# The last 64 keys' scores of two heads: one matmul over the whole array, or one per head in half of the array

## The chip, the cores and the metric

The kernel runs on one core of one Trainium2 chip. The metric is the device time of the program in microseconds (us), the median of several runs; smaller is better. The engines go by the names of the profile: PE is TensorE's matmul part, PEld its weight loads (they overlap PE), ACT is ScalarE, DVE is VectorE, POOL is GpSimd, SP is the engine that issues most transfers. SBUF is the working memory; PSUM is the memory that TensorE writes its results to, in eight banks of 512 f32 values per partition.

## The reference

Two stages, all in f32. The first is attention with 8 batches, 8 heads, 576 positions and head size 64, in which every query keeps only its 32 largest scores:

```
scores = scale * np.matmul(q, k.transpose(0, 1, 3, 2))
kth = np.partition(scores, -top_k, axis=-1)[..., -top_k:-top_k + 1]
scores = np.where(scores >= kth, scores, -1000000000.0)
attn = softmax(scores)          # max subtracted, 1e-9 added to the sum
out = np.matmul(attn, v)
```

The second is an MLP over the 4608 rows of 512 values which that gives: x times w_in (512 x 2048), the exact gelu, times w_out (2048 x 512).

## The kernel before

**Tiles.** Two heads form a pair, 32 pairs in all. The 576 positions are four blocks of 128 and a last part of 64 (TL). An item is one block of 128 queries of one pair (128 items), or the last 64 queries of two pairs together (16 items, t == NM). For each pair, transpose_qk (L238) puts q and k, transposed, into a tile qk: partitions 0 to 63 hold head 0, partitions 64 to 127 head 1. Columns KT and up hold the first 512 keys of both heads. Columns SM + P to KT are the last keys: 128 columns, where the first 64 belong to head 0 and the other 64 to head 1. The raw tile was zero outside the two heads' own corners, so in those columns head 0's rows are zero for head 1's keys and the other way round.

**Scores (L280).** For an item of 128 queries, TensorE makes t_ps at L290: one matmul over all 128 rows of the array, whose 128 columns are the last-key scores of both heads at once, thanks to the zeros. Then L294 makes s_ps, two PSUM banks, one per head: four matmuls of 256 columns, each over the 64 rows of its head, so that two heads can go through the two halves of the array at the same time. An f32 matmul is two passes in the trace, each with its own weight load. ScalarE then copies s_ps (L298, 1024 columns) and t_ps (L299, 128 columns) into the item's score tile s in SBUF, with the scale. The row of s is laid out as head 0's 512 keys, head 0's last 64, head 1's last 64, head 1's 512 keys, so that each head's 576 scores are in one piece.

**The loop (L609).** One trip per item, with several items in different stages: scores of item n + 2, the product with V of item n - 3 (attend, L440, matmuls at L458 or L468 into the tile o), the softmax of item n - 1 on ScalarE (L380 and L381), transposes of the weights of item n - 2 (tp_t at L409, two tp at L427, copied by ScalarE at L410 and L434), top_k of item n on VectorE (L341, L344), and the normalisation of item n - 1 on POOL (L392). Between these stand pieces of the MLP (mlp, L576): l1_piece (L499, h_ps), the gelus on ScalarE (L513), l2_piece (L534, y_ps), and the copy of a finished y (L548). In a trip with attend, which is every second trip for the items of 128 queries, the matmuls of o follow those of the scores directly; else a piece of the MLP follows.

**What sets the order.** Each engine runs its instructions in the order of this program text (manual_schedule). Semaphores make one engine wait for another, and all that stands behind a waiting instruction on its engine waits too.

**PSUM.** The eight banks are: two for s_ps (tag "s", one buffer), two for the tag "tp", two for h_ps and two for y_ps. The tag "tp" is shared by t_ps, o, the transposes tp_t, tp and tp_qk:

```
s_ps = ps.tile([P, 2, 512], f32, tag="s", bufs=1, name="s_ps")
t_ps = ps.tile([P, 512], f32, tag="tp", name="t_ps")
...
o = ps.tile([P, 512], f32, tag="tp", name="o")
```

Each new tile of a tag takes the bank of the tile that came two before it, and its first matmul waits until that one's last reader is done.

Of the kernel before, what the change touches and what calls it, by code (L numbers as in the profile page):

```python
# [14 lines left out]
def kernel(  # L15
# [19 lines left out]
    nc = tc.nc  # L35
    f32, i32, u32 = mybir.dt.float32, mybir.dt.int32, mybir.dt.uint32
    bf16, i16, u16 = mybir.dt.bfloat16, mybir.dt.int16, mybir.dt.uint16
    AF = mybir.ActivationFunctionType
    ALU = mybir.AluOpType

    B, H, S, D = q.shape
    P = 128
# [5 lines left out]
    SM = NM * P  # L48
    TL = S - SM
# [6 lines left out]
    scale = 1.0 / float(D) ** 0.5  # L56
# [5 lines left out]
    ps = ctx.enter_context(tc.tile_pool(name="ps", bufs=2, space=bass.MemoryType.PSUM))  # L62
# [172 lines left out]
    KT = SM + 2 * P  # L235
# [31 lines left out]
    def spread(t, step, n):  # L267

        return bass.AP(tensor=t.tensor, offset=t.offset, ap=[list(t.ap[0]), [step, 2], [1, n]])

    def half(r, e):


        return slice((r ^ e) * TL, ((r ^ e) + 1) * TL)
# [5 lines left out]
    def scores(i):  # L280
        if i >= N:
            return
        pair, t = items[i]
        S_of[i] = s = work.tile([P, 2 * S], f32, tag="s", bufs=5, name="s")
        s_ps = ps.tile([P, 2, 512], f32, tag="s", bufs=1, name="s_ps")
        t_ps = ps.tile([P, 512], f32, tag="tp", name="t_ps")
        if t < NM:
            qk = qk_of[pair]
            lhsT = qk[:, t * P : (t + 1) * P]
            nc.tensor.matmul(t_ps[:, 0:P], lhsT=lhsT, rhs=qk[:, SM + P : KT], start=True, stop=True)  # L290
            for c in range(2):
                for e in range(2):
                    rows = slice(e * D, (e + 1) * D)
                    nc.tensor.matmul(  # L294
                        s_ps[:, e, c * 256 : (c + 1) * 256], lhsT=lhsT[rows, :],
                        rhs=qk[rows, KT + c * 256 : KT + (c + 1) * 256], start=True, stop=True,
                    )
            nc.scalar.activation(spread(s, S + TL, SM), s_ps, func=AF.Copy, scale=scale)  # L298
            nc.scalar.activation(s[:, SM : S + TL], t_ps[:, 0:P], func=AF.Copy, scale=scale)  # L299
        else:  # L300
            for r in range(2):
                qk = qk_of[pair + r]
                for e in range(2):
                    nc.tensor.matmul(
                        t_ps[half(r, e), r * TL : (r + 1) * TL],
                        lhsT=qk[:, SM + e * TL : SM + (e + 1) * TL],
                        rhs=qk[:, SM + P + e * TL : SM + P + (e + 1) * TL],
                        start=True, stop=True,
                    )

            for r in range(2):
                qk = qk_of[pair + r]
                for e in range(2):
                    rows = slice(e * D, (e + 1) * D)
                    nc.tensor.matmul(  # L315
                        s_ps[half(r, e), r, :], lhsT=qk[rows, SM + e * TL : SM + (e + 1) * TL],
                        rhs=qk[rows, KT:], start=True, stop=True,
                    )
            s2 = s.rearrange("p (r n) -> p r n", r=2)
            nc.scalar.activation(s2[:, :, 0:SM], s_ps, func=AF.Copy, scale=scale)  # L320
            nc.scalar.activation(
                s2[:, :, SM:S], t_ps[:, 0:P].rearrange("p (r n) -> p r n", r=2),
                func=AF.Copy, scale=scale,
            )
# [270 lines left out]
    for pair in range(2):  # L595
        for piece in transpose_qk(pair, pair == 0):
            piece()
        if pair == 0:
            scores(0)
            scores(1)  # L600
# [8 lines left out]
    for n in range(ahead):  # L609

        left[0] = 7 if n < START + 2 * NP else 8
        weights_add(unit_in(n))
        scores(n + 2)
        product = attend(n - 3)
        late = n > START
# [71 lines left out]
```

## Time and profile before

| what | value |
|---|---|
| time, median of 3 runs | 1713.43 us (1713.32 to 1719.77) |
| PE busy | 1612.4 us, 94% |
| DVE busy | 1428.2 us, 83% |
| ACT busy | 1189.2 us, 69% |
| L290, t_ps | 256 passes, 53.4 us |
| L294, s_ps | 1024 passes, 154.5 us |
| L298, copy of s_ps | 128 times, 1028 ns each |
| L299, copy of t_ps | 128 times, 278 ns each |
| L548, copy of y | 36 times, 603 ns each |

How to read the profile: busy time is the time in which an engine has an instruction running, and matmuls overlap one another, so their busy times do not add up to the time they cost; the distance from one group's start to the next group's start does. A line of the table of groups names the source line, the engine, the tiles (out<-in), the shape, how often, then the busy time and the mean of one. A line of the table of waits reads "engine tile line <- who ended the wait: us in total, times, longest". A line of the timeline is start, length, engine, line, operation, tiles and how many were merged; in brackets stands the idle time before it and what ended it.

### The profile page before, as it was taken

How to read it: one execution, taken by the hardware profiler on the slowest of the kernel's cores; microseconds unless marked ns; L12 is line 12 of the kernel's file. 1: busy time of each engine (PE TensorE's matmuls, PEld its weight loads, DVE VectorE, ACT ScalarE, POOL GpSimd, SP SyncE). 2: the span in 40 equal slices, each digit the busy share in tenths (PEclk: the TensorE clock that was granted, in tenths of full speed). 3: DMA queues.
4: the chain of work that ended last, by engine and by line, in shares of the span. 5: the costliest groups of instructions: out<-in, count | busy, mean ns of one | idle time of the engine just before them, and what ended most of it. 6: DMA issues, size and time to landing. Idle time of an engine off the chain costs nothing.

```text
span 1713.1 us, 24404 instructions
## 1 busy us (share of the span) xinstructions
PE 1612.4 (94%) x8480; PEld 1093.2 (64%) x8480; DVE 1428.2 (83%) x3042; ACT 1189.2 (69%) x2147; POOL 663.0 (39%) x764
## 2 busy tenths in 40 slices
PE   5558999999999999999999999999999999999999
PEld 3336567766666667666666667676666666766665
DVE  6998989988799887998889888898889987899900
ACT  5877876767676767776767776776777776777730
POOL 3667833333233332333333323333333333333310
PEclk8669999999999999999999999999999999999999
DMA  5422210011100111002100011001110010000000
GB/s 157 133 99 87 84 48 1 13 27 24 40 13 1 41 29 41 1 13 49 28 27 1 27 42 41 1 14 27 29 48 1 13 29 15 21 1 13 7 13 13
DMA packets 126715, 56.10 MB, mean 33 GB/s; under 512 B 117888, under 2 KB 117888, under 8 KB 126592
## 3 DMA queue, kind: packets, MB, share of 16 engines
q1 hardware_dynamic: 125056, 52.16, 11.4%
q0 software_dynamic: 320, 2.10, 0.3%
q8 instruction: 67, 1.10, 0.3%
q14 instruction: 56, 0.46, 0.1%
q10 hardware_dynamic: 1216, 0.30, 0.1%
HBM read 45.08 MB, written 9.44 MB: 32 GB/s over the span
## 4 chain that ended last, share of the span: by engine, by line
PE 83%; ACT 6%; POOL 0%; issue 0%; ACTq 0%; POOLq 0%
PE h_ps L506 27%; PE y_ps L542 27%; PE o L458 8%; PE s_ps L294 7%; PE tp L427 6%; PE o L468 2%; PE t_ps L290 1%; PE tp_qk L249 1%; ACT s L381 1%; ACT L381 1%; ACT s L380 1%; PE s_ps L315 1%; PE tp_t L409 1%; ACT L517 1%; ACT g L517 1%; ACT pt L434 0%
## 5 line engine op out<-in xcount | busy, mean ns | idle before, releaser
L341 DVE MAX8 top<-rest 128x8 f32<-128x576 f32 x864 | 612.5, 754 | 0.0
L506 PE MATMUL h_ps<-xT,w_in_sb 128*128 128x256 f32 (+1 forms) x2560 | 559.3, 363 | 4.3 <-ACT g L517 4.3
L542 PE MATMUL y_ps<-w_out_sb,g 128*128 128x512 f32 x1152 | 546.1, 598 | 0.0
L392 POOL TENSOR_SCALAR s<-s,rden 128x576 f32<-128x576 f32 x288 | 493.6, 1723 | 0.8 <-issue 0.4
L506 PEld LDWEIGHTS h_ps<-xT,w_in_sb 128*128 128x128 f32 x2560 | 430.3, 192 | 66.6 <-issue 15.8
L344 DVE MATCH_REPLACE8 rest<-top,rest 128x576 f32<-128x576 f32 x576 | 425.4, 750 | 0.0
L373 POOL TENSOR_SCALAR den<-den 128x2 f32<-128x2 f32 x144 | 32.0, 222 | 884.0 <-ACT s L381 883.4
L542 PEld LDWEIGHTS y_ps<-w_out_sb,g 128*128 128x128 f32 x1152 | 196.2, 190 | 173.2 <-issue 172.7
L298 ACT ACTIVATE s<-s_ps 128x1024 f32<-128x1024 f32 x128 | 131.6, 1028 | 189.7 <-PE s_ps L294 189.7
L381 ACT ACTIVATE s<-s,bias 128x576 f32<-128x576 f32 x288 | 223.3, 775 | 12.8
L380 ACT ACTIVATE s<-s,neg 128x576 f32<-128x576 f32 x288 | 223.8, 777 | 1.6 <-POOL neg L356 1.1
L434 ACT COPY pt<-tp 128x512 f32<-128x512 f32 x256 | 147.3, 576 | 109.2 <-PE tp L427 108.5
L427 PEld LDWEIGHTS tp<-ident,s 128*128 128x128 f32 x1152 | 147.0, 145 | 118.5 <-issue 57.6
L344 DVE MATCH_REPLACE8 rest<-top,s 128x576 f32<-128x576 f32 x288 | 212.4, 748 | 0.0
L341 DVE MAX8 top<-s 128x8 f32<-128x576 f32 x288 | 202.4, 747 | 5.1 <-ACT s L299 5.1
L427 PE MATMUL tp<-ident,s 128*128 128x128 f32 x1152 | 179.6, 281 | 28.3 <-ACT qk L253 13.7
L367 DVE RECIPROCAL rden<-den 128x2 f32<-128x2 f32 x144 | 23.7, 164 | 194.2 <-POOL den L373 194.2
L294 PE MATMUL s_ps<-qk 64*128 64x256 f32 x1024 | 154.5, 423 | 3.5 <-ACT s L298 3.5
L458 PE MATMUL o<-pt,raw_v 128*64 128x256 f32 x1280 | 153.6, 387 | 2.1 <-ACT pt L434 2.1
L458 PEld LDWEIGHTS o<-pt,raw_v 128*64 128x64 f32 x1280 | 86.8, 138 | 66.9 <-issue 17.9
L294 PEld LDWEIGHTS s_ps<-qk 64*128 64x128 f32 x1024 | 92.9, 196 | 27.1 <-ACT s L298 4.0
L517 ACT ACTIVATE g<-h_ps 128x512 f32<-128x512 f32 x144 | 78.6, 595 | 37.8 <-PE h_ps L506 37.1
(65 smaller groups left out, 1106.6 us busy)
## 6 DMA issues: line engine op xcount, KB each, us to landing
raw_q<-in_q_dram SPq DMA_DIRECT2D x64, 128.0 KB, 2.3
raw_v<-in_v_dram SPq DMA_DIRECT2D x64, 128.0 KB, 2.4
out_dram<-y SPq DMA_DIRECT2D x32, 256.0 KB, 2.2
raw_k<-in_k_dram SPq DMA_DIRECT2D x62, 128.0 KB, 2.4
w_out_sb<-in_moe_w_in_dram SPq DMA_DIRECT2D x12, 511.8 KB, 4.7
w_out_sb<-in_moe_w_out_dram SPq DMA_DIRECT2D x10, 511.8 KB, 4.0
w_out_sb<-in_moe_w_in_dram POOLq DMA_DIRECT2D x4, 511.8 KB, 8.6
words<-in_moe_w_out_dram SPq DMA_DIRECT2D x4, 511.8 KB, 5.0
```

The lines of the kernel that those rows point to most:

```text
L294: nc.tensor.matmul(s_ps[:, e, c * 256 : (c + 1) * 256], lhsT=lhsT[rows, :], rhs=qk[rows, KT + c * 256 : KT + (c + 1) * 256], start=True, s ...
L298: nc.scalar.activation(spread(s, S + TL, SM), s_ps, func=AF.Copy, scale=scale)
L341: nc.vector.max(st["top"][:, e, 8 * r : 8 * r + 8], cur[e])
L344: nc.vector.match_replace(rest[:, e], st["top"][:, e, 8 * r : 8 * r + 8], cur[e], LOWEST)
L380: nc.scalar.activation(s, s, func=AF.Prelu, bias=st["neg"][:, e, 1:2], scale=1.0, alpha=STEEP)
L381: nc.scalar.activation(s, s, func=AF.Exp, bias=st["bias"][:, e : e + 1], scale=1.0, accum_out=st["den"][:, e : e + 1],)
L392: nc.gpsimd.tensor_scalar(s, s, st["rden"][:, e : e + 1], None, op0=ALU.mult)
L427: nc.tensor.transpose(tp[:, j * P : (j + 1) * P], s[:, first + j * P : first + (j + 1) * P], ident)
L434: nc.scalar.copy(out=dst, in_=tp.rearrange("p (j n) -> p j n", j=NM))
L458: nc.tensor.matmul(o[e * D : (e + 1) * D, 0:n], lhsT=vt[:, j, e, :], rhs=pt[:, e * NM + j if j < NM else 2 * NM, :], start=(j == 0), stop= ...
L506: nc.tensor.matmul(h_tile(u)[:, i, :], lhsT=w_in_sb[:, ko, f * P : (f + 1) * P], rhs=xT[:, ko, c0 : c0 + n], start=(ko == 0), stop=(ko == ...
L542: nc.tensor.matmul(y_of[sub], lhsT=g_of[u][:, i, sub * P : (sub + 1) * P], rhs=w_out_sb[:, f, :], start=(f == 0), stop=(f == FT - 1),)
```

## The change

The scores of the last keys are made per head. Each head's 64 columns come from a matmul over the 64 rows of that head alone, so all six matmuls of an item use one half of the array. Two halves may not write one PSUM bank at the same time, so each head's tail has a bank of its own: t_ps for head 0, the new t1_ps for head 1, both from the tag "tp". The order on TensorE is head 0's tail, then the four mains beginning with head 1 and alternating, then head 1's tail, so that the two halves have the same work. ScalarE makes three copies in place of two: head 0's tail first, then the 1024 columns of s_ps, then head 1's tail. It is meant to use both halves fully: the whole-array matmul, half of whose products are with zeros, goes away. Items of the last 64 queries (t == NM) are as before.

```diff
-            nc.tensor.matmul(t_ps[:, 0:P], lhsT=lhsT, rhs=qk[:, SM + P : KT], start=True, stop=True)
-            for c in range(2):
-                for e in range(2):
-                    rows = slice(e * D, (e + 1) * D)
-                    nc.tensor.matmul(
-                        s_ps[:, e, c * 256 : (c + 1) * 256], lhsT=lhsT[rows, :],
-                        rhs=qk[rows, KT + c * 256 : KT + (c + 1) * 256], start=True, stop=True,
-                    )
+            t1_ps = ps.tile([P, 512], f32, tag="tp", name="t_ps")
+            tails = [
+                (e, dst[:, 0:TL], SM + P + e * TL, TL) for e, dst in enumerate((t_ps, t1_ps))
+            ]
+            mains = [
+                (e, s_ps[:, e, c * 256 : (c + 1) * 256], KT + c * 256, 256)
+                for c in range(2) for e in (1, 0)
+            ]
+            for e, dst, at, n in tails[:1] + mains + tails[1:]:
+                rows = slice(e * D, (e + 1) * D)
+                nc.tensor.matmul(
+                    dst, lhsT=lhsT[rows, :], rhs=qk[rows, at : at + n], start=True, stop=True
+                )
+            nc.scalar.activation(s[:, SM:S], t_ps[:, 0:TL], func=AF.Copy, scale=scale)
             nc.scalar.activation(spread(s, S + TL, SM), s_ps, func=AF.Copy, scale=scale)
-            nc.scalar.activation(s[:, SM : S + TL], t_ps[:, 0:P], func=AF.Copy, scale=scale)
+            nc.scalar.activation(s[:, S : S + TL], t1_ps[:, 0:TL], func=AF.Copy, scale=scale)
```

## The prediction, made before the changed kernel ran

> **What bounds the kernel now.** I read the page's busy times and slices first, then the waits of each engine, then the timeline around single score tiles.
>
> ```profile
> PE 1612.4 (94%) x8480; PEld 1093.2 (64%) x8480; DVE 1428.2 (83%) x3042; ACT 1189.2 (69%) x2147; POOL 663.0 (39%) x764
> ...
> PE   5558999999999999999999999999999999999999
> ...
> DVE  6998989988799887998889888898889987899900
> ACT  5877876767676767776767776776777776777730
> ```
>
> From slice 6 on (about 215 us) TensorE (PE) is full. Before that VectorE (DVE) is: the table of windows gives it 43.00 us busy in 43:86 and again in 86:129. So after 215 us a stop of TensorE lengthens the run; from 43 to 129 it does not, as long as VectorE is fed. That the later part does not hang on VectorE is in its waits, the first of these lines; the second tells how often ScalarE (ACT) is early or late for the scores.
>
> ```profile
> DVE rden L367 <- POOL den L373: 194.2, 98, 8.7
> ...
> ACT s L298 <- PE s_ps L294: 189.7, 97, 5.2
> ```
>
> VectorE waits 194.2 us in all. ScalarE waited for TensorE at 97 of the 128 score evictions; at the other 31 it arrived late. What it was doing then is in the timeline. First a tile where a gelu stood ahead of the scores, ScalarE from 674 us (the scores began on TensorE at 674.49):
>
> ```profile
> 674.76 1.08 ACT L517 ACTIVATE g<-h_ps 128x512 f32<-128x512 f32 x2
> 676.05 1.02 ACT L298 ACTIVATE s<-s_ps 128x1024 f32<-128x1024 f32 x1 [0.20 <-PE s_ps L294]
> 676.97 0.27 ACT L299 ACTIVATE s<-t_ps 128x128 f32<-128x128 f32 x1
> ```
>
> Then a tile where a finished output y was copied too, on both engines:
>
> ```profile
> 651.35 1.08 ACT L517 ACTIVATE g<-h_ps 128x512 f32<-128x512 f32 x2
> 652.32 1.08 ACT L548 COPY y<-y_ps 128x512 f32<-128x512 f32 x2
> 653.26 1.07 ACT L298 ACTIVATE s<-s_ps 128x1024 f32<-128x1024 f32 x1
> ```
>
> ```profile
> 650.66 0.59 PE L542 MATMUL y_ps<-w_out_sb,g 128*128 128x512 f32 x1
> 651.09 0.38 PE L290 MATMUL t_ps<-qk 128*128 128x128 f32 x2
> 651.40 1.14 PE L294 MATMUL s_ps<-qk 64*128 64x256 f32 x8
> 652.47 2.50 PE L468 MATMUL o<-ptt,raw_v 128*128 128x128 f32 x20
> ```
>
> The reader is to see this: TensorE goes from the scores (651.09) to the product with V (o, 652.47) after 1.38 us and does not care that ScalarE reaches these scores only at 653.26. In the first case it reaches them at about 675.84 (end of the second gelu), 1.35 us after the scores began.
>
> **What the skill says, and the trace.** "TensorEngine Tiling (Array Packing)", Key Properties: a change of the tiling mode drains TensorE. The trace agrees: from t_ps (128 rows) to s_ps (64 rows) takes 0.31 us where two passes of 128 columns need 2 x 0.109 (four transposes of L427 take 0.44 until the next group starts), so 0.09 is drain. The same page, Gotcha 1: different row tiles cannot use one PSUM bank at once; that is why each head's tail now needs its own bank. "TensorE: Matmul & The Clock Gate", LDWEIGHTS: the load takes columns/1.2 ns, 107 ns for 128 columns, however few rows. The pitch of 0.109 us agrees, though matmul and load need the same time there, so it does not tell them apart.
>
> **The change, part by part.**
>
> TensorE's work. The page counts 256 instructions at L290 for 128 tiles, so an f32 matmul is two passes, each with its own weight load. Before: two passes of 128 columns, 0.218; drain 0.096; then from 651.40 to o at 652.47, 1.065: the eight L294 passes run as four pairs of the two row halves, 4 x 0.216 = 0.864 (0.216 is the pitch of 256 columns: L506's four in 0.87), and the 0.20 left I split into the first weight load, which nothing hides behind a drain, 0.104, and the drain out, 0.097. Sum 1.379; the timeline has 1.38. After: no 128-row matmul, six 64-row ones. The mode changes stay two, only the first stands before the tails. Each half now carries one tail of two passes plus two mains of two. A tail pass streams 64 columns, 0.054, but its successor's 128-column load needs 0.107 and can start only as the pass starts. I take 0.107 per tail pass, and 0.054 and a full serialisation as the ends. One half: 2 x 0.107 + 4 x 0.216 = 1.078; with drain in 0.096, first load 0.104, drain out 0.097: 1.375. So TensorE gains 0.004 us per tile, 0.5 us in all: the removed full-array matmul comes back as loads.
>
> ScalarE's work. One 128x128 eviction (278 ns at L299) becomes two of 128x64. "ScalarE: Activation LUTs", What ACT_TABLE_LOAD costs, gives 186 ns + 0.833 ns per element, 239 at 64; at 128 it gives 293 where the trace has 272 median, so I scale from the trace: 272 - 53 = 219. That is 0.16 us more per tile, 20 us over 128 tiles, of which nearly all lies in ScalarE's idle time: the first tail's eviction goes ahead of the wait for s_ps. After the mains only one of 219 stands where one of 272 stood.
>
> The buffers. This is the part that costs. The tag "tp" has two banks, and each new tile of it takes the bank of the tile before last. Before: scores took one (A), and the o after it took B, last read by the copy at L434, which ScalarE had done before the gelu. After: scores take A and B, o takes A, so o waits for the eviction of the first tail. That eviction is queued on ScalarE behind the gelus and y copies of the block before. Behind o, in TensorE's order, stand all later matmuls, so nothing fills the wait. From ScalarE's end to TensorE's start a release takes 0.05 (timeline, the copy at L253 to L427).
>
> How long, tile by tile after 215 us. o stands straight behind these scores in 64 cases, and alternates with tiles that have MLP pieces first (next user of "tp" 2.3 us or more after the start, against about 0.9 for the first tail's eviction: no wait). In twelve of the 64 ScalarE is not late. 34 have only gelus: the eviction starts at 1.35 - 0.115 (a copy starts that much ahead of the end of the gelu before it: 652.32 against 652.43) = 1.237 after the start, ends at 1.456, o starts at 1.51 in place of 1.375: 0.13 each, 4.5 us. 18 have y copies (36 of 603 ns in the table of groups, four of them after the last scores): in 14 with two of them the eviction starts at 653.26 - 651.09 = 2.17, o at 2.45: 1.07 each, 15.0 us; in 4, with one, at 1.70, o at 1.97: 0.59 each, 2.3 us. Together 22 us. After the delayed o ScalarE waits for o anyway (L474 idle 0.50 in the y case), so the next tile starts equally late and nothing is made up.
>
> Before 215 us ScalarE is late by 2 to 4 us at most tiles (weight conversion), and o waits up to 2 us five times; four of these fall in windows where VectorE is full, the one at 150 us can cost up to 2. I take 1.
>
> The second bank's wait, tail 1 on the last L434 copy, is hidden by the four mains ahead of it and by MLP pieces. Result: 1713.4 - 0.5 + 22 + 1 = 1736.
>
> **Rivals.**
> 1. Tail passes cost only their 64 columns (0.054). Then a tile is 0.107 shorter where o does not wait for ScalarE: some 60 tiles, 6 us; where it waits, the time of o is ScalarE's. 1736 - 6 = 1730. For it: L304, 64 columns with 64-column loads, runs its pairs fast. Against: those loads are half as wide.
> 2. The halves do not overlap once they are out of step: about 0.13 more per tile, again only where o does not wait: 1736 + 8 = 1744. For it: pairs ran in step in the trace before. Against: four quarter tiles at L315 overlap freely, eight passes of 512 columns in 1.02 us.
> 3. No net wait: o's stop is taken from waits TensorE has anyway. Time 1714. For it: TensorE's waits add up to 97 us. Against: 42 of them are L409 on POOL before 170 us, and what recurs later (L427 on L253, 2.1 us a time) stands in the few tiles with a new pair's transposes.
> 4. Faster: rival 1 on all 128 tiles and no wait for the tail bank, 1713.4 - 13.7 = 1700. It needs two of my steps wrong.
>
> **How the numbers follow.** Main case 0.62, rival 1 0.13, rival 2 0.12, rival 3 0.08, rival 4 0.05. Slower by over 0.5% (above 1722) is the main case and rivals 1 and 2, 0.87; same 0.08; faster 0.05. The range runs from rival 1 less some microseconds for the eviction's length and the release, 1725, to rival 2 plus the early phase's 2 us, 1747; rivals 3 and 4 stay outside with 0.13.
>
> **What would show it.** In the waits of TensorE: o at L458 and L468 behind the new first tail's eviction, about 50 times after 215 us, 22 us, the longest 1.1. Timeline from the first tail to o: 1.38 us where ScalarE is free, 1.5 behind gelus, 2.4 behind y copies. A tile's six matmuls as long as the five before means the load bound holds; 1.27 means rival 1, 1.5 everywhere rival 2. VectorE's wait at L367 grows. I am wrong if o starts at 1.38 behind a late ScalarE, or if TensorE's later waits shrink by as much as these grow.

## The result, and the profile after

The changed kernel takes 1742.77 us (median of 5 runs, 1738.42 to 1743.92), the kernel before 1714.55 beside it. The ratio is 1.0154, with a 95% interval of 1.0133 to 1.0176: slower by about 28 us. In the changed kernel the six matmuls of an item stand at L302, the three copies at L305 (first tail), L306 (s_ps) and L307 (second tail). All lines behind them moved by 8: o is now L466 and L476, the MLP's L514 and L550, the gelu L525, the copy of y L556.

The busy times of the page hardly tell what happened. TensorE is as full as before, in a longer span:

```profile
PE 1619.0 (93%) x8736; PEld 1102.1 (63%) x8736; DVE 1428.5 (82%) x3042; ACT 1203.1 (69%) x2275; POOL 662.5 (38%) x764
...
PE   5558999999999999999999999999999999999999
```

The table of waits does (engine, tile and line <- who ended the wait: us in total, times, longest). TensorE's, of the kernel after:

```profile
PE o L466 <- ACT s L305: 21.4, 19, 2.5
...
PE o L476 <- ACT s L305: 4.2, 4, 1.1
```

No such line was there before. The 25.6 us count only stops that outlast the modelled end of the last matmul; short ones show in the weight loader, where o waits for L305 57 times.

VectorE's waits took up what TensorE lost, 223.3 us where there were 194.2, so VectorE was not what held the kernel:

```profile
DVE rden L375 <- POOL den L381: 223.3, 101, 8.7
```

The timeline of one tile with two y copies, the counterpart of the one shown before, first ScalarE, then TensorE (start, length, engine, line):

```profile
661.93 1.08 ACT L525 ACTIVATE g<-h_ps 128x512 f32<-128x512 f32 x2
662.90 1.08 ACT L556 COPY y<-y_ps 128x512 f32<-128x512 f32 x2
663.84 0.27 ACT L305 ACTIVATE s<-t_ps 128x64 f32<-128x64 f32 x1
663.95 1.07 ACT L306 ACTIVATE s<-s_ps 128x1024 f32<-128x1024 f32 x1
```

```profile
661.75 0.32 PE L302 MATMUL t_ps<-qk 64*128 64x64 f32 x1
...
662.02 0.86 PE L302 MATMUL s_ps<-qk 64*128 64x256 f32 x6
...
662.78 0.27 PE L302 MATMUL t_ps<-qk 64*128 64x64 f32 x1
664.16 2.50 PE L476 MATMUL o<-ptt,raw_v 128*128 128x128 f32 x20 [1.06 <-ACT s L305]
```

TensorE has its last score matmul under way at 662.78 and stands until 664.16, 0.05 after the first tail's copy ends at 664.11. ScalarE came to that copy only after the gelus and the copies of y. Where ScalarE is free, the same distance, from the first tail to o, is 1.28 us (650.07 to 651.35):

```profile
650.07 0.32 PE L302 MATMUL t_ps<-qk 64*128 64x64 f32 x1
...
651.35 2.50 PE L476 MATMUL o<-ptt,raw_v 128*128 128x128 f32 x20
```

Over the run after 215 us the distance takes four values: 1.28 where ScalarE is free, 1.43 behind gelus (34 times), 1.92 behind gelus and one copy of y (4 times), 2.41 behind two (14 times). One tile, at 224 us, stands apart: it waits 2.1 us for the copy at L442, as its counterpart before waited for that at L434.

### The profile page after: what moved, and what is told of

It reads as the page before. It is cut to its first block, busy times and chain, and to the rows that moved or that the text cites. A ratio compares the mean times of both kernels' runs of the same rounds, so it can differ in the third digit from the quotient of the medians.

```text
span 1741.4 us, 25044 instructions
## 1 busy us (share of the span) xinstructions
PE 1619.0 (93%) x8736; PEld 1102.1 (63%) x8736; DVE 1428.5 (82%) x3042; ACT 1203.1 (69%) x2275; POOL 662.5 (38%) x764
## 3 DMA queue, kind: packets, MB, share of 16 engines
q8 instruction: 69, 1.13, 0.3%
## 4 chain that ended last, share of the span: by engine, by line
PE 66%; ACT 20%; issue 2%; POOL 0%; ACTq 0%; POOLq 0%
PE h_ps L514 27%; PE y_ps L550 17%; PE o L466 8%; PE tp L435 5%; ACT L525 4%; ACT g L525 3%; ACT pt L442 3%; PE s_ps L302 3%; ACT s L389 3%; ACT s L388 3%; PE o L476 2%; PE tp_qk L249 1%; PE t_ps L302 1%; ACT L389 1%; ACT y L556 1%
## 5 line engine op out<-in xcount | busy, mean ns | idle before, releaser
L514 PE MATMUL h_ps<-xT,w_in_sb 128*128 128x256 f32 (+1 forms) x2560 | 559.8, 363 | 5.5 <-ACT g L525 5.5
L550 PE MATMUL y_ps<-w_out_sb,g 128*128 128x512 f32 x1152 | 546.1, 598 | 0.0
L514 PEld LDWEIGHTS h_ps<-xT,w_in_sb 128*128 128x128 f32 x2560 | 430.6, 192 | 67.7 <-issue 19.4
L550 PEld LDWEIGHTS y_ps<-w_out_sb,g 128*128 128x128 f32 x1152 | 196.2, 190 | 162.6 <-issue 156.5
L389 ACT ACTIVATE s<-s,bias 128x576 f32<-128x576 f32 x288 | 223.3, 775 | 13.0
L442 ACT COPY pt<-tp 128x512 f32<-128x512 f32 x256 | 147.4, 576 | 110.2 <-PE tp L435 109.5
L375 DVE RECIPROCAL rden<-den 128x2 f32<-128x2 f32 x144 | 23.1, 160 | 223.3 <-POOL den L381 223.3
L302 PE MATMUL s_ps<-qk 64*128 64x256 f32 x1024 | 182.4, 417 | 1.0 <-ACT s L306 1.0
L466 PE MATMUL o<-pt,raw_v 128*64 128x256 f32 x1280 | 155.7, 390 | 23.8 <-ACT s L305 21.4
L306 ACT ACTIVATE s<-s_ps 128x1024 f32<-128x1024 f32 x128 | 131.7, 1029 | 43.3 <-PE s_ps L302 43.0
L302 PEld LDWEIGHTS t_ps<-qk 64*128 64x128 f32 x512 | 90.1, 196 | 80.9 <-issue 57.2
L466 PEld LDWEIGHTS o<-pt,raw_v 128*64 128x64 f32 x1280 | 87.8, 139 | 80.9 <-ACT s L305 33.0
L302 PEld LDWEIGHTS s_ps<-qk 64*128 64x128 f32 x1024 | 119.6, 197 | 6.6 <-ACT s L306 1.4
```

The lines of the kernel that those rows point to most:

```text
L302: nc.tensor.matmul(dst, lhsT=lhsT[rows, :], rhs=qk[rows, at : at + n], start=True, stop=True)
L389: nc.scalar.activation(s, s, func=AF.Exp, bias=st["bias"][:, e : e + 1], scale=1.0, accum_out=st["den"][:, e : e + 1],)
L442: nc.scalar.copy(out=dst, in_=tp.rearrange("p (j n) -> p j n", j=NM))
L466: nc.tensor.matmul(o[e * D : (e + 1) * D, 0:n], lhsT=vt[:, j, e, :], rhs=pt[:, e * NM + j if j < NM else 2 * NM, :], start=(j == 0), stop= ...
L514: nc.tensor.matmul(h_tile(u)[:, i, :], lhsT=w_in_sb[:, ko, f * P : (f + 1) * P], rhs=xT[:, ko, c0 : c0 + n], start=(ko == 0), stop=(ko == ...
L550: nc.tensor.matmul(y_of[sub], lhsT=g_of[u][:, i, sub * P : (sub + 1) * P], rhs=w_out_sb[:, f, :], start=(f == 0), stop=(f == FT - 1),)
```

## The experiments

Three explanations had to be told apart. The theory: the second tail takes a bank of the tag "tp", so that o gets the bank of the first tail and waits for its copy on a late ScalarE. Rival A: ScalarE's third copy costs by itself. Rival B: the half-array matmuls cost by themselves. Each ratio below is taken against runs of the kernel before made beside the experiment; their median stands with it.

**The matmuls alone.** Edit against the changed kernel:

```diff
-            nc.scalar.activation(s[:, SM:S], t_ps[:, 0:TL], func=AF.Copy, scale=scale)
             nc.scalar.activation(spread(s, S + TL, SM), s_ps, func=AF.Copy, scale=scale)
-            nc.scalar.activation(s[:, S : S + TL], t1_ps[:, 0:TL], func=AF.Copy, scale=scale)
+            nc.scalar.activation(s[:, SM : S + TL], s_ps[:, 0, 0:P], func=AF.Copy, scale=scale)
```

> Keeps the six half-array matmuls in their two tail banks, but ScalarE copies as in the kernel before: s_ps, then one copy of 128 columns, taken from s_ps in place of the tails. The tails' scores are thus left out of the result; the work of every engine is else that of the change. The second bank is free as soon as it is written. Theory (o waits for the first tail's copy, behind a late ScalarE): no wait of o, 1714 us, within 3 of the kernel before. Rival A (ScalarE's third copy costs): also 1714. Rival B (the half-array matmuls cost): 1743, as the changed kernel.

Measured: 1717.31 against 1713.65 us, ratio 1.0013 (1.0000 to 1.0025). Rival B is out as the cause: by the ratio the matmuls cost 2 us, at most 4, of the 28. In the trace not even these look to be theirs: the distance from the first tail to o is 1.28 us in 63 of the 64 tiles after 215 us. The trace has four stretches of 3.41 us after 215 us in which TensorE ran at half its clock, where that of the kernel before has one (more on such stretches below). No wait of o for a copy of the scores is left in TensorE's table; the one line on o is this:

```profile
PE o L465 <- ACT pt L441: 1.3, 1, 1.3
```

**The copies alone.** Edit against the kernel before:

```diff
+            nc.scalar.activation(s[:, SM:S], t_ps[:, 0:TL], func=AF.Copy, scale=scale)
             nc.scalar.activation(spread(s, S + TL, SM), s_ps, func=AF.Copy, scale=scale)
-            nc.scalar.activation(s[:, SM : S + TL], t_ps[:, 0:P], func=AF.Copy, scale=scale)
+            nc.scalar.activation(s[:, S : S + TL], t_ps[:, TL:P], func=AF.Copy, scale=scale)
```

> The matmuls and the one bank of the kernel before; only the tail's copy is cut in two of 64 columns, the first ahead of the copy of s_ps. Theory: ScalarE's 20 us more lie in its idle time, o takes the bank that was free before: 1714 to 1716. Rival A: 1730 to 1743. Rival B: 1714.

Measured: 1713.25 against 1713.65 us, ratio 1.0001 (0.9993 to 1.0008). Rival A is out. The two small copies are there, at 231 and 227 ns, but they lie in time in which ScalarE waited: the wait ahead of the scores' copies is now in two parts.

```profile
ACT s L298 <- PE t_ps L290: 111.4, 59, 3.7
...
ACT s L299 <- PE s_ps L294: 51.7, 63, 1.9
```

163.1 us where the kernel before had 189.7.

**The bank alone, first attempt.** The copies of the tail and of s_ps change places, and one more tile is taken:

```diff
+            ps.tile([P, 512], f32, tag="tp", name="t_ps")
...
+            nc.scalar.activation(s[:, SM : S + TL], t_ps[:, 0:P], func=AF.Copy, scale=scale)
             nc.scalar.activation(spread(s, S + TL, SM), s_ps, func=AF.Copy, scale=scale)
-            nc.scalar.activation(s[:, SM : S + TL], t_ps[:, 0:P], func=AF.Copy, scale=scale)
```

> The matmuls of the kernel before, two copies as before but the 128 columns of the tail ahead of s_ps; and one more tile of the tag tp is taken in each score tile and never used, so that o gets the bank of t_ps. Theory: o waits for that copy as in the changed kernel, behind gelus 0.2 us, behind y copies 1.15: 1740 to 1748. Rivals A and B: 1714.

Measured: 1713.28 against 1713.65 us, ratio 0.9996 (0.9987 to 1.0004): a miss, but no evidence against the theory. Its trace has no wait of o for the tail, which fits that the unused tile got no bank and o went where it had gone before. The run is of use as a control: to copy the tail ahead of s_ps costs nothing by itself.

**The banks swapped.** The tile t1_ps is taken ahead of t_ps in the changed kernel:

```diff
+        if t < NM:
+            t1_ps = ps.tile([P, 512], f32, tag="tp", name="t_ps")
         t_ps = ps.tile([P, 512], f32, tag="tp", name="t_ps")
...
-            t1_ps = ps.tile([P, 512], f32, tag="tp", name="t_ps")
```

> The changed kernel with the two tail banks taken in the other order, so that o gets the bank of the tail that is copied last. Theory: every o that stands behind scores waits for the last copy: about 1.3 us more where ScalarE is free (12 times), 1.15 behind gelus (33), 1.03 behind y copies (18), 72 us in all: 1800 to 1820. Rivals A and B: 1743, since no work is added.

Measured: 1738.89 against 1713.65 us, ratio 1.0143 (1.0129 to 1.0156), as the change itself. Again the edit did not do what I meant: the trace still shows o behind the first tail's copy (L304 here). With the run before it this fits that a tile gets its bank at its first use, not where it is taken; and the first tail is still written first.

```profile
PE o L465 <- ACT s L304: 20.6, 19, 2.0
```

**The bank alone, with a tile that is used.** Edit against the kernel before:

```diff
+            nc.scalar.activation(s[:, SM : S + TL], t_ps[:, 0:P], func=AF.Copy, scale=scale)
             nc.scalar.activation(spread(s, S + TL, SM), s_ps, func=AF.Copy, scale=scale)
-            nc.scalar.activation(s[:, SM : S + TL], t_ps[:, 0:P], func=AF.Copy, scale=scale)
+            pad = ps.tile([P, 512], f32, tag="tp", name="pad")
+            nc.scalar.copy(out=pad[:, 0:2], in_=ident[:, 0:2])
```

> As the run of the bank alone, but the second tile of the tag is used (ScalarE writes two columns of it after the scores), since a tile that no instruction touches got no bank: in this program o goes to the bank of t_ps. Matmuls as before the change, the 128 columns of the tail copied ahead of s_ps. Theory: o waits for that copy as in the changed kernel: 1738 to 1748. Rivals A (ScalarE's third copy) and B (half-array matmuls): 1714.

Measured: 1742.61 against 1717.26 us, ratio 1.0153 (1.0131 to 1.0174). The whole loss is there without one half-array matmul and with the tail copied in one piece. From the first attempt, which lost nothing, this kernel differs in the tile that is used and ScalarE's copy of two columns into it; that a third small copy on ScalarE costs nothing was shown by the copies alone. Its waits of o are those of the change:

```profile
PE o L460 <- ACT s L298: 23.8, 20, 2.3
...
PE o L470 <- ACT s L298: 4.4, 4, 1.1
```

**The first tail copied last.** This is what the swap of banks was to show. In the changed kernel the copy of t_ps goes behind the other two:

```diff
-            nc.scalar.activation(s[:, SM:S], t_ps[:, 0:TL], func=AF.Copy, scale=scale)
             nc.scalar.activation(spread(s, S + TL, SM), s_ps, func=AF.Copy, scale=scale)
             nc.scalar.activation(s[:, S : S + TL], t1_ps[:, 0:TL], func=AF.Copy, scale=scale)
+            nc.scalar.activation(s[:, SM:S], t_ps[:, 0:TL], func=AF.Copy, scale=scale)
```

> The changed kernel with the copy of the first tail moved behind the two others on ScalarE; no work is added. Theory: o, which goes to that tail's bank, waits for all three copies: about 1.3 us more where ScalarE is free (12 times), 1.15 behind gelus (33), 1.03 behind y copies (18), 72 us in all: 1800 to 1820. Rivals A and B: 1743.

Measured: 1845.81 against 1717.26 us, ratio 1.0753 (1.0730 to 1.0776). No work was added, a copy was moved, and 103 us more were lost than by the change. The time is above the 1800 to 1820 expected. The waits of o are now

```profile
PE o L466 <- ACT s L306: 80.9, 53, 2.8
...
PE o L476 <- ACT s L306: 23.3, 16, 2.0
```

104.2 us in place of 25.6, which is 78.6 more. The distance from the first tail to o became 2.64 where ScalarE is free or behind gelus, 2.84 behind one copy of y and 3.33 behind two: 1.36, 1.21 and 0.92 more, where I had 1.3, 1.15 and 1.03. Tile by tile that is 73 us after 215 us, so the 72 expected came true. The traces of the two kernels differ by 102 us. Of the other 29, 10 arise before 215 us. Most of what is left goes with the clock: after 215 us this trace has 13 stretches of 3.41 us at half the clock, that of the changed kernel has two. At some 1.7 us each, an estimate from those measured below, eleven more cost 18 us. Other users of the tag wait longer too (transposes of a new pair behind L306 8.2 us, tp_t behind L307 8.0), but their waits add little after 215 us.

**o ahead of the scores.** In the changed kernel:

```diff
-        scores(n + 2)
         product = attend(n - 3)
+        scores(n + 2)
```

> The changed kernel with the product with V ahead of the scores in each trip, so that ScalarE has the 2.3 us of o to finish its gelus and copies before the first tail is there. Theory: the waits of o for a tail go; the scores reach ScalarE 2.3 us later, so the softmax starts about 0.8 us later in these trips, which VectorE's waits should take up: 1714 to 1728. Rivals A (third copy) and B (half-array matmuls): 1743, since all work stays.

Measured: 1739.81 against 1714.11 us, ratio 1.0134 (1.0112 to 1.0155). The waits of o for a tail are gone from the table, as the theory has it, and yet the time is not back. The same move in the kernel before tells why:

> The kernel before with the product with V ahead of the scores, as the run that put o first did for the changed kernel. If that run's 25 us came from the order alone, this one is slow as well, 1735 to 1740. If they come from the two tail banks, whose next users now wait for the scores' copies in the trips with a new pair's transposes, this one is at 1710 to 1716.

Measured: 1751.59 us, ratio 1.0203 (1.0181 to 1.0226), with its own runs of the kernel before at 1717.26. The order costs by itself, more than the wait that it takes away, so these two runs say nothing against the theory, and my expectation for the first was wrong. Besides, they show where half-array tails pay. The tiling mode of a group, the rows and columns of the array that one matmul uses, stands ahead of its tiles' sizes in the timeline. With o first, what stands ahead of the scores is often in the mode 128*64, and the old order of scores then changes mode once more: into 128*128 for t_ps, then into 64*128. The changed kernel goes to 64*128 at once. First the kernel before with o first, then the changed one:

```profile
730.16 2.38 PE L458 MATMUL o<-pt,raw_v 128*64 128x256 f32 x20
732.47 0.49 PE L290 MATMUL t_ps<-qk 128*128 128x128 f32 x2
732.89 1.13 PE L294 MATMUL s_ps<-qk 64*128 64x256 f32 x8
733.95 0.38 PE L506 MATMUL h_ps<-xT,w_in_sb 128*128 128x128 f32 x1
```

```profile
721.19 2.38 PE L466 MATMUL o<-pt,raw_v 128*64 128x256 f32 x20
723.50 0.32 PE L302 MATMUL t_ps<-qk 64*128 64x64 f32 x1
...
724.78 1.49 PE L514 MATMUL h_ps<-xT,w_in_sb 128*128 128x128 f32 x11
```

From the start of o to the group behind the scores it is 3.79 us and 3.59. The 0.20 recurs behind every o in the mode 128*64 after 215 us but one, 47 times, together 9.4 of the 12 us between the two runs. Behind an o in the mode 128*128 (L468 and L476, 16 trips) both kernels take about 3.61. What the order itself costs was not taken apart further.

**The gelus one piece sooner.** In the changed kernel, so that ScalarE is less late:

```diff
-    GELU_AT = 5
+    GELU_AT = 4
```

> The changed kernel with GELU_AT 4 in place of 5: the gelus go to ScalarE one piece of the MLP sooner, ahead of the last transposes' copy, so that ScalarE comes to the scores about 0.7 us earlier. Theory: no wait of o behind gelus, about 0.4 left behind two y copies, the early part's 4 us stay: 1720 to 1730. Rivals A and B: 1743.

Measured: 1850.14 against 1717.26 us, ratio 1.0777 (1.0752 to 1.0802). My expectation failed. The gelus now stand ahead of the last copy of a trip's transposes (L442), and TensorE waits for that copy's bank as it starts the scores. One wait was traded for a larger one, and its trace has 17 stretches of 3.41 us at half the clock after 215 us, where the changed kernel's has two. So this run cannot tell how the lateness of ScalarE scales the loss:

```profile
PE t_ps L302 <- ACT pt L442: 54.9, 45, 1.2
...
PE o L466 <- ACT s L305: 14.8, 19, 1.9
```

## Why the prediction was right

**The bank, the main step.** Right, and shown by two runs: the bank without the matmuls gives the whole loss, the matmuls without the bank's copies none that matters. The count was right as well (14, 4 and 34 tiles). The sizes were a little low: 0.15 for 0.13 behind gelus, 1.13 for 1.07 behind two y copies, 0.64 for 0.59 behind one. Sum 23 us for 22. In the y case I had taken 0.219 us for a 64-column copy; there it takes 0.27, and 0.224 in the median.

**Nothing made up.** Right. A transpose of the last trips, at 1639.33 us before, starts at 1667.60 after, 28.3 later; one at 215.31 starts at 219.55, 4.2 later. So 24 of the 28 us come after 215 us, and the waits of o account for 23 of them. What is left is the clock, for which the prediction had no term. Twice after 215 us the changed kernel's TensorE ran 3.41 us at half its clock (from 369.31 and 1280.67 us), the kernel before once (from 454.03); each time it fell back by about 1.7 us. In the windows (columns: stretch, its length, busy us of PE, PEld, DVE, ACT and POOL with counts, granted clock as a share of the full one, DMA share, GB/s), first after, then before:

```profile
369.40:372.60 3.20, 3.20 (x12) 2.74 (x13) 0.97 (x2) 2.13 (x4) 0.00 (x0) 0.50 0.00 0
```

```profile
454.10:457.30 3.20, 3.20 (x12) 2.56 (x11) 1.00 (x4) 2.55 (x5) 0.95 (x4) 0.50 0.00 0
```

These are the profiled executions; in others their number may differ.

**TensorE's work.** Right: I had 1.375 us in place of 1.379. Measured: the drain in, 0.096 (L550's six passes to L302 2.67 where 2.577 was usual), then 1.28, so 1.376. The sign that I had given, 1.38 from the first tail to o and 1.27 for rival 1, was set wrong: in the new order the drain lies ahead of the first tail, so from there my own sum is 1.279 and rival 1's is 1.17. The 1.28 measured is mine. In trips without a wait of o nothing was gained or lost, three apart that gained 0.20. That the first half's tail passes are bound by their weight loads fits the timeline of the y case: t_ps at 661.75, the first main of its half (merged into the line at 662.02) at 662.08, 0.33 later: two loads of 0.107 and the 0.104 or so that the first load costs. Rival 1 would have had 0.21 there. The two halves, out of step by a tail, did not slow each other, which is against rival 2.

**ScalarE's work.** Right, shown by the copies alone.

**The part before 215 us.** Here is most of the miss, 4.2 us where I took 1. The step that failed is "the one at 150 us can cost up to 2. I take 1". o waits there 1.89 us, at the bound I gave, and then runs slowly. The windows of the kernel after:

```profile
151.90:154.00 2.10, 0.31 (x3) 0.17 (x2) 2.10 (x3) 2.07 (x4) 2.04 (x2) 1.00 0.00 0
154.00:158.20 4.20, 4.10 (x21) 2.26 (x21) 4.20 (x11) 1.08 (x3) 4.12 (x3) 0.59 0.01 4
```

After the stop the granted clock of TensorE is 0.59 for the stretch, and the product o takes 4.07 us; before, it took 2.38 at the full clock:

```profile
151.60 2.38 PE L458 MATMUL o<-pt,raw_v 128*64 128x256 f32 x20
```

The Trainium skill, "TensorE: Matmul & The Clock Gate", HAM oscillation, gives as the rule no idle gaps of TensorE above about 3.4 us. Here a stop of 1.89 us was enough, and the measurement decides. The other runs bear this out: where o stops at this place for 1.89 to 2.06 us (banks swapped, bank alone with a used tile, gelus sooner), 3.4 us at half the clock follow; where it does not stop (matmuls alone, copies alone, first attempt), the clock stays at 1.00. The four other late tiles before 130 us cost nothing that lasted: at 126 us the changed kernel was 0.36 us behind, since VectorE was the bound there.

So the forecast of 1736 fell short by 7 us: some 3 from the early part, 1 from the sizes of the waits, 1.1 since the kernel before itself measured higher in these runs, and 1 to 2 from one more stretch at half the clock. The last comes from single traces, the 7 from medians.

**A version better than both** did not come of it. Both tails in one bank would free o, but the two halves' matmuls would then write one bank with nothing to order them. That was not tried.

## What to carry to other kernels

Before adding a tile to a shared PSUM tag, list who takes its banks next and which copy frees them: a matmul that was free of ScalarE may come to stand behind everything ScalarE has queued. Splitting a copy off for an early start does not help if the engine that makes it is late just then. A matmul of few columns over half the array need not be cheaper: here a tail's two passes cost the time of their weight loads, and they paid only where they saved a change of tiling mode. When two runs differ by more than the waits explain, compare the granted clock along both traces.

## What the hardware showed beyond that

- Passes of the two row halves of the array start independently: in the y case s_ps of one half starts at 661.76 beside the other half's tail at 661.75, and at the end t_ps of one and s_ps of the other both start at 662.72, with no loss against the sum for one half (1.376 measured, 1.375 worked out).
- One more change of tiling mode costs 0.20 us a time (3.79 in place of 3.59, 47 times). An estimate of its parts: 0.10 until the array is drained, from 2.67 less 2.577, and the other 0.10 for a first weight load that nothing hides.
- A stop of 1.89 us was followed by 3.4 us at half the clock, which nearly doubled its cost. Not every stop of that length is: in the changed kernel nine stops of 1.7 to 2.2 us lie between 150 and 1300 us, and three were followed so (from 154.27, 369.31 and 1280.67). These three starts lie whole multiples of 3.413 us apart (63 and 267 of them), and unlike the other six stops, the three hardly cross a mark of that grid. What decides was not tested.
